# Splitting the first up-weight load over two queues in a state-space plus gated-MLP kernel

## The chip, the cores and the metric

The kernel runs on one core of a Trainium2 chip. The metric is device time in microseconds (us) of one execution; the figure for a kernel is the median of several runs. The core's engines are TensorE (PE in the profile, its weight loads PEld), VectorE (DVE), ScalarE (ACT), GpSimd (POOL) and SyncE (SP). DMA loads here are issued by SP and by ScalarE (SPq and ACTq in the profile).

## The reference

Everything is bfloat16 at the edges. For x of 2048 tokens by 512 channels:

```
xn = layernorm(x)                                   # per token, eps 1e-5
A  = S5(xn):  Bu = xn @ B_bar.T                     # complex, 512 states
              h[t] = Lam_bar * h[t-1] + Bu[t]       # a scan over 2048 tokens
              y = 2 * Re(h @ C.T) + xn * Dskip
B  = (gelu(xn @ w_gate) * (xn @ w_up)) @ w_down     # 512 -> 1376 -> 512
out = x + A + B
```

`Lam_bar` and `B_bar` are made from the small parameters `log_dt`, `Lambda_re` and `Lambda_im` (512 numbers each).

## The kernel before

Tokens are worked in four blocks of 512, a block in four tiles of 128. The program records every operation with the buffers that it reads and writes, and a planner (`Sched`) sets the order on VectorE, ScalarE and GpSimd from estimated durations. TensorE and SP keep the order in which the code records them. `emit` then writes out each engine's list with the semaphore waits. `order_behind(op, prev)` tells the planner to put `op` behind `prev`.

**The start.** Block 0 is treated specially, because weights and tokens arrive while it is worked. Its four x tiles are loaded one by one (`ld_x0`). The gate weights `WG` and up weights `WU` come in four chunks of columns (0 to 384, to 640, to 896, to 1376). The first gate chunk comes as two loads of 192 KB, for channels 0 to 255 and 256 to 511 (`ld_wg0`, line 490): the first on SP, the second on ScalarE's queue. The first up chunk is one load of 384 KB on SP. SP issues in this order: x of tile 0, gate half 0, x of tile 2, the up chunk, x of tile 3, then the other chunks, then the transpose of the parameters (`tr_par`, line 511), four transposes of block 0's normalised tiles (`TR(0)`, line 711), x of block 1, and the transposing loads of B. ScalarE's queue issues x of tile 1, gate half 1 and the three parameter loads (`load_par`, line 507), and then its first arithmetic: the mean of tile 1 (line 926).

**Work on block 0.** VectorE takes each tile's statistics and subtracts the mean (line 921, for tile 1 line 929 with ScalarE's mean). TensorE transposes the centred tile (`cent_T`, line 662), ScalarE (once VectorE too, if the letters say so) copies the transpose to memory (line 669). Then `GT_mm` (line 687) multiplies a tile by a part of the gate or up columns. Parts are 192, 192, 256 and 256 columns wide; part 0 and part 1 make up the first chunk. A product has four matmuls, one for each 128 channels (`ks`); `us` is [0] for gate, [1] for up. Gate and up of one part lie beside each other in one PSUM bank. `GT_evac` applies gelu with the tile's scale on ScalarE (line 696) and multiplies by the up half on VectorE (line 699).

For tiles 0 and 1 the order on TensorE is: gate of tile 0 for the first two channel blocks, both parts; the same for the last two; a few filler matmuls (line 909); gate of tile 1, both parts; up of tile 0 part 0; the transpose of tile 2; up of tile 0 part 1; up of tile 1, both parts. Tile 2 and the rest follow with gate and up together. ScalarE's list behind this has: gelu of tile 0 part 0, copy of tile 2's transpose, gelu of tile 0 part 1, and so on.

**The rest.** Blocks go through the gate and up products (`GU`, line 812), the input projection of the scan (`BU`, line 723), the scan and its rotations on VectorE (`CHAIN`), and the output products (`DN`, line 853). `BU(1)` follows `BU(0)` on TensorE and needs the four transposes of block 1.

Of the kernel before, what the change touches and what calls it, by code (L numbers as in the profile page):

```python
# [77 lines left out]
class Sched:  # L78
# [95 lines left out]
    def _backward(self, span):  # L174
        ops = self.ops
        left = {op.id: len(op.users) for op in ops}
        late = {op.id: span for op in ops}
        ready = {e: [] for e in ENGINES}
        last = {e: [op for op in ops if op.eng == e] for e in INORDER}
        for op in ops:  # L180
            if left[op.id] == 0 and op.eng not in INORDER:
                ready[op.eng].append(op)
        busy = {e: span for e in ENGINES}
        begin = {}
        n = len(ops)
        while n:
            best = None
            for e in ENGINES:
                if e in INORDER:
                    if not last[e] or left[last[e][-1].id]:  # L190
                        continue
                    op = last[e][-1]
                else:
                    if not ready[e]:
                        continue
                    op = max(ready[e], key=lambda o: (min(busy[e], late[o.id]), o.finish, o.id))
                end = late[op.id] if op.kind == "dma" else min(busy[e], late[op.id])
                if best is None or end > best[0]:
                    best = (end, op)
            end, op = best  # L200
            e = op.eng
            if e in INORDER:
                last[e].pop()
            else:
                ready[e].remove(op)
            begin[op.id] = end - op.dur
            if op.kind == "dma":
                begin[op.id] = min(begin[op.id], busy[e] - op.issue)
                busy[e] = begin[op.id]
            else:  # L210
                busy[e] = begin[op.id]
            n -= 1
            for d in op.deps:
                late[d.id] = min(late[d.id], begin[op.id] - LAT(d, op))
                left[d.id] -= 1
                if left[d.id] == 0 and d.eng not in INORDER:
                    ready[d.eng].append(d)
        return begin

    def _forward(self, prio):  # L220
        ops = self.ops
        free_at = {e: 0.0 for e in ENGINES}
        dma_pipe = 0.0
        ndeps = {op.id: len(op.deps) for op in ops}
        ready = {e: [] for e in ENGINES}
        queue = {e: [op for op in ops if op.eng == e] for e in INORDER}
        qpos = {e: 0 for e in INORDER}
        for op in ops:
            if ndeps[op.id] == 0 and op.eng not in INORDER:
                ready[op.eng].append(op)  # L230
        order = {e: [] for e in ENGINES}
        nleft = len(ops)

        def rdy_time(op):
            return max([d.finish + LAT(d, op) for d in op.deps] + [op.nb])

        while nleft:
            best = None
            for e in ENGINES:
                if e in INORDER:  # L240
                    if qpos[e] >= len(queue[e]):
                        continue
                    op = queue[e][qpos[e]]
                    if ndeps[op.id] != 0:
                        continue
                    st = max(free_at[e], rdy_time(op))
                else:
                    if not ready[e]:
                        continue
                    cands = [(max(free_at[e], rdy_time(op)), op) for op in ready[e]]  # L250
                    st0 = min(c[0] for c in cands)
                    stb, b = min(cands, key=lambda c: (prio[c[1].id], c[1].id))
                    if stb <= st0 + 150.0:
                        st, op = stb, b
                    else:
                        limit = max(stb, prio[b.id])
                        fill = [c for c in cands if c[1] is not b and
                                c[0] + (c[1].issue if c[1].kind == "dma" else c[1].dur) <= limit]
                        if fill:
                            f0 = min(c[0] for c in fill)  # L260
                            fill = [c for c in fill if c[0] <= f0 + 150.0]
                            st, op = min(fill, key=lambda c: (prio[c[1].id], c[1].id))
                        else:
                            st, op = stb, b
                if best is None or st < best[0]:
                    best = (st, op)
            st, op = best
            e = op.eng
            if e in INORDER:
                qpos[e] += 1  # L270
            else:
                ready[e].remove(op)
            op.start = st
            if op.kind == "dma":
                free_at[e] = st + op.issue
                xfer = op.dur - 2000.0
                t0 = max(st, dma_pipe) if xfer > 10.0 else st
                dma_pipe = max(dma_pipe, t0 + xfer)
                op.finish = t0 + xfer + 2000.0
            else:  # L280
                op.finish = st + op.dur
                free_at[e] = op.finish
            order[e].append(op)
            nleft -= 1
            for u in op.users:
                ndeps[u.id] -= 1
                if ndeps[u.id] == 0 and u.eng not in INORDER:
                    ready[u.eng].append(u)
        return order, max(op.finish for op in ops)

    def emit(self):
# [19 lines left out]
        for e in ENGINES:  # L311
            seen = {}
            prog = []
            for op in order[e]:
                need = {}
                for d in op.deps:
                    if d.kind == "eng" and d.eng == e and (e == "tensor" or d is op.behind):
                        continue
                    key = ("e", d.eng) if d.kind == "eng" else ("d", d.id)
                    if seen.get(key, 0) >= d.val:  # L320
# [35 lines left out]
def d_dve_ts4x(n): return 220.0 + 0.26 * n  # L356
D_TINY = 160.0
def d_act(n, ptr=0): return 190.0 + 0.833 * n + 90.0 * ptr
# [3 lines left out]
def build(nc, ins, out):  # L362
    with ExitStack() as es:
# [121 lines left out]

        def ld_x0(j, queue="sync", after=()):
            return S.dma(lambda e, j=j: e.dma_start(X[j].ap, x2[128 * j:128 * (j + 1), :]), 128 * 1024, writes=[X[j]], tag="ld_x0", queue=queue, after=after)
        WG0h = [Buf("WG0h%d" % n, "sbx", n / 2, (n + 1) / 2) for n in range(2)]

        def ld_wg0(n, queue, after=()):  # L490
            return S.dma(lambda e: e.dma_start(WG.ap[:, 2 * n:2 * n + 2, 0:384],
                                        ins["B_w_gate"][256 * n:256 * (n + 1), 0:384].rearrange("(k p) f -> p k f", p=128)),
                  192 * 1024, writes=[WG0h[n]], tag="ld_w", queue=queue, after=after)
        ld_x0(0)
        S.order_behind(ld_x0(1, "scalar", [wrm]), GATE["table"])
        ld_wg0(0, "sync")
        S.order_behind(ld_wg0(1, "scalar", [wrm]), GATE["table"])
        ld_x0(2)
        ld_w(WU, WUc, ins["B_w_up"], 0)
        ld_x0(3)  # L500
        for ci in (1, 2):
            ld_w(WG, WGc, ins["B_w_gate"], ci)
            ld_w(WU, WUc, ins["B_w_up"], ci)

        def load_par():
            for q, nm in enumerate(("A_log_dt", "A_Lambda_re", "A_Lambda_im")):
                S.dma(lambda e, q=q, nm=nm: e.dma_start(PROW.ap[4 * q:4 * q + 4, :], ins[nm].rearrange("(s p) -> s p", p=128)),
                      1024, writes=[PROWq[q]], tag="ld_" + nm, queue="scalar", after=[half])

        def tr_par():  # L510
            S.dma(lambda e: e.dma_start_transpose(PAR.ap.rearrange("p q t -> p (q t)").unsqueeze(1), PROW16.ap), 4096,
# [163 lines left out]
        def GT_mm(j, r, bank, us, ks=range(KD)):  # L675
# [1 line left out]
            w = f1 - f0  # L677
            ci = max(0, r - 1)
            Wc = [(WGc, WUc)[u][ci] for u in us]
            if ci == 0 and us == [0] and len(ks) == 2:  # L680
                Wc = [WG0h[ks[0] // 2]]
            dst = PS[bank][:, w * us[0]:w * (us[-1] + 1)].rearrange("p (w f) -> p w f", w=len(us))

            def f(e):
# [235 lines left out]
        def sub(j):  # L920
            return V(lambda e: e.tensor_scalar(XN[j].ap, X[j].ap, MVt[0][j].ap[:, 0:1], None, ALU.subtract),
                     d_dve_ts4x(512), [X[j], MVt[0][j]], [XN[j]], "sub")
        load_par()
        load_W()
        tr_par()
        ACT(lambda e: e.activation(H0[3].ap[:, 0:D], X[1].ap, ACTF.Copy, scale=-1.0 / D, accum_out=NM1.ap), d_act(512) + 90,
            [X[1]], [H0[3], NM1], "mean1")
        ch(*stats(0, 0)); ch(sub(0))
        ch(V(lambda e: e.tensor_scalar(XN[1].ap, X[1].ap, NM1.ap, None, ALU.add), d_dve_ts4x(512), [X[1], NM1], [XN[1]], "sub"))
        ch(*stats(0, 1))  # L930
# [24 lines left out]
            GT_evac(j, r, bank, rss[j])  # L955
        for r in range(2):
            GT_mm(1, r, ub[1, r], [0])
        for j in range(2):
            for r in range(2):
                GT_mm(j, r, ub[j, r], [1])  # L960
                GT_evac(j, r, ub[j, r], rss[j])
                if j == 0 and r == 0:
                    cent_T(2, tb)
# [100 lines left out]
```

## Time and profile before

| | us |
|---|---|
| median of 6 runs | 177.92 (177.64 to 178.01) |
| the profiled execution | 177.93 |
| its span, first to last instruction | 176.2 |
| TensorE busy | 172.8 (98%) |
| VectorE busy | 162.4 (92%) |
| ScalarE busy | 90.3 (51%) |
| GpSimd busy | 9.7 (6%) |

The profile lists instructions in time order (start and length in us, engine, source line, operation, tiles), with the idle time before one in brackets and what ended it. The chain is the sequence of work that ended last, followed back from the last instruction. A window row gives, for a stretch of time, its length, the busy time of PE, PEld, DVE, ACT and POOL (with instruction counts), the granted TensorE clock, the DMA share and GB/s. Matmuls overlap: one that is 0.25 us long can follow another after 0.08 us, so the distance of starts is what counts. Times below are from the start of the span.

### The profile page before, as it was taken

How to read it: one execution, taken by the hardware profiler on the slowest of the kernel's cores; microseconds unless marked ns; L12 is line 12 of the kernel's file. 1: busy time of each engine (PE TensorE's matmuls, PEld its weight loads, DVE VectorE, ACT ScalarE, POOL GpSimd, SP SyncE). 2: the span in 40 equal slices, each digit the busy share in tenths (PEclk: the TensorE clock that was granted, in tenths of full speed). 3: DMA queues.
4: the chain of work that ended last, by engine and by line, in shares of the span. 5: the costliest groups of instructions: out<-in, count | busy, mean ns of one | idle time of the engine just before them, and what ended most of it. 6: DMA issues, size and time to landing. Idle time of an engine off the chain costs nothing.

```text
span 176.2 us, 2489 instructions
## 1 busy us (share of the span) xinstructions
PE 172.8 (98%) x876; PEld 84.7 (48%) x891; DVE 162.4 (92%) x283; ACT 90.3 (51%) x169; POOL 9.7 (6%) x25
## 2 busy tenths in 40 slices
PE   8999999999999999999999999999999999999995
PEld 3854464444644444444644444444464444444454
DVE  6978999986999999979999999999999999999981
ACT  5476568899876899002676793000667790000000
POOL 3212030210000000011000000000000000000000
PEclk9999999999999999999999999999999999999999
DMA  5996996974997000012015000002101000000141
GB/s 162 316 311 152 207 234 130 133 139 102 240 290 165 4 0 0 2 41 78 4 34 113 4 0 0 4 0 77 42 0 30 4 0 0 0 0 0 33 149 61
DMA packets 33396, 14.36 MB, mean 81 GB/s; under 512 B 23688, under 2 KB 33384, under 8 KB 33384
## 3 DMA queue, kind: packets, MB, share of 16 engines
q1 hardware_dynamic: 32944, 13.87, 34.5%
q10 hardware_dynamic: 440, 0.33, 0.7%
q8 instruction: 7, 0.11, 0.3%
q14 instruction: 5, 0.04, 0.1%
HBM read 6.46 MB, written 2.10 MB: 49 GB/s over the span
## 4 chain that ended last, share of the span: by engine, by line
PE 98%; issue 0%; DVE 0%
PE PS L853 37%; PE PS L812 32%; PE PS L723 16%; PE PS L687 7%; PE PS L786 3%; PE PS L902 2%; PE PS L662 1%; PE PS L909 0%; DVE arena L871 0%
## 5 line engine op out<-in xcount | busy, mean ns | idle before, releaser
L853 PE MATMUL PS<-arena 128*128 128x512 bf16 (+3 forms) x317 | 65.9, 367 | 0.3
L812 PE MATMUL PS<-arena 128*128 128x512 bf16 x258 | 57.5, 380 | 0.3
L853 PEld LDWEIGHTS PS<-arena 128*128 128x128 bf16 (+1 forms) x323 | 30.8, 98 | 35.2
L812 PEld LDWEIGHTS PS<-arena 128*128 128x128 bf16 x264 | 25.8, 98 | 30.4
L756 DVE TENSOR_TENSOR_SCAN arena<-arena 128x512 bf16<-128x512 f32 x32 | 38.8, 1255 | 0.0
L827 ACT ACTIVATE arena<-PS 128x512 bf16<-128x512 f32 x33 | 19.8, 599 | 37.0 <-PE PS L812 33.4
L723 PE MATMUL PS<-arena 128*128 128x512 bf16 x125 | 27.8, 380 | 0.2
L831 ACT ACTIVATE arena<-PS 128x512 bf16<-128x512 f32 x33 | 19.7, 597 | 4.8 <-PE PS L812 4.6
L845 ACT ACTIVATE PS<-arena 128x512 f32<-128x512 bf16 (+2 forms) x17 | 9.6, 581 | 20.4 <-PE PS L853 19.7
L723 PEld LDWEIGHTS PS<-arena 128*128 128x128 bf16 x128 | 12.5, 98 | 14.9
L727 ACT ACTIVATE arena<-PS 128x512 bf16<-128x512 f32 x32 | 17.6, 594 | 2.3 <-PE PS L723 2.3
L871 DVE TENSOR_TENSOR arena<-PS,arena 128x512 bf16<-128x512 f32 (+2 forms) x17 | 10.8, 652 | 5.0 <-PE PS L853 4.5
L833 DVE TENSOR_TENSOR arena<-arena 128x512 bf16<-128x512 bf16 x33 | 13.0, 418 | 1.7 <-ACT arena L831 1.6
L687 PE MATMUL PS<-arena 128*128 128x192 bf16 (+2 forms) x80 | 13.2, 320 | 0.0
L613 DVE BATCH_NORM_STATS2 arena<-arena 128x6 f32<-128x512 bf16 x16 | 10.3, 684 | 0.8 <-DMA arena<-in_A_x_dram 0.8
L743 DVE TENSOR_TENSOR arena<-arena 128x4096 bf16<-128x4096 bf16 (+1 forms) x5 | 9.2, 1861 | 0.5 <-ACT arena L608 0.5
L687 PEld LDWEIGHTS PS<-arena 128*128 128x128 bf16 x80 | 7.3, 100 | 5.0 <-DMA arena<-in_B_w_up_dram 0.3
L745 DVE TENSOR_TENSOR arena<-arena 128x4096 bf16<-128x4096 bf16 (+1 forms) x5 | 9.2, 1859 | 0.4 <-ACT arena L609 0.4
L696 ACT ACTIVATE arena<-PS,arena 128x192 bf16<-128x192 f32 (+1 forms) x16 | 6.7, 447 | 5.0 <-PE PS L687 4.2
L768 DVE TENSOR_TENSOR arena<-arena 128x4096 bf16<-128x4096 bf16 x4 | 9.2, 2289 | 0.1
L769 DVE TENSOR_TENSOR arena<-arena 128x4096 bf16<-128x4096 bf16 x4 | 9.1, 2285 | 0.0
L699 DVE SCALAR_TENSOR_TENSOR arena<-PS,arena 128x192 bf16<-128x192 f32 (+1 forms) x16 | 6.6, 444 | 0.9 <-ACT arena L696 0.7
(84 smaller groups left out, 110.4 us busy)
## 6 DMA issues: line engine op xcount, KB each, us to landing
out_dram<-arena SPq DMA_DIRECT2D x15, 128.0 KB, 1.7
arena<-in_A_x_dram SPq DMA_DIRECT2D x3, 512.0 KB, 4.9
arena<-in_B_w_down_dram SPq DMA_DIRECT2D x1, 1280.0 KB, 8.1
arena<-in_B_w_gate_dram SPq DMA_DIRECT2D x2, 256.0 KB, 5.6
arena<-in_B_w_up_dram SPq DMA_DIRECT2D x2, 256.0 KB, 5.8
arena<-in_B_w_gate_dram SPq DMA_DIRECT2D x1, 480.0 KB, 5.8
arena<-in_B_w_up_dram SPq DMA_DIRECT2D x1, 480.0 KB, 5.9
arena<-arena SPq DMA_TRANSPOSE x25, 2.5
```

The costliest lines, as they stand in the source:

```text
L613: return (V(lambda e: e.bn_stats(ST[tt].ap, X[tt].ap), d_dve_1x(512), [X[tt]], [ST[tt]], "bnst"), V(lambda e: e.bn_aggr(MVt[b][j].ap, ST[t ...
L687: ins_ = e.matmul(dst, XCd(j, k), WGU[:, us[0]:us[-1] + 1, k, f0:f1], start=(k == 0), stop=(k == KD - 1))
L723: ins_ = e.matmul(PS[bank][:, :], BBT[c][dk].ap[:, 128 * s:128 * (s + 1)], XNT[b].ap[:, dk, :], start=(dk == 0), stop=(dk == KD - 1))
L727: GATE["evBu"] = ACT(lambda e, bank=bank, k3=k3, s=s, c=c: e.activation(SSc[k3][s][c].ap, PS[bank][:, :], ACTF.Copy), d_act(512), [BANK[ba ...
L756: V(lambda e, g=g, rb=rb, init=init: e.tensor_tensor_scan(g.ap, rb, g.ap, init, ALU.mult, ALU.add), d_dve_scan(512), [g, PA[RRr]] + ([CARc ...
L812: ins_ = e.matmul(PS[bank][0:m, c0:c1], W.ap[:, dk, 128 * ft:128 * ft + m], XNT[b].ap[:, dk, c0:c1], start=(dk == 0), stop=(dk == KD - 1))
L827: GATE["last_gelu"] = ACT(lambda e, bg=bg, kk=kk, m=m: e.activation(GG[kk].ap[0:m, :], PS[bg][0:m, :], ACTF.Gelu_apprx_tanh), d_act(512), ...
L831: ACT(lambda e, bu=bu, kk=kk, m=m: e.activation(UPB[kk].ap[0:m, :], PS[bu][0:m, :], ACTF.Copy), d_act(512), [BANK[bu]], [UPB[kk]], "evU")
L833: V(lambda e, kk=kk, m=m, ft=ft, k2=k2: e.tensor_tensor(HTt[k2][ft].ap[0:m, :], GG[kk].ap[0:m, :], UPB[kk].ap[0:m, :], ALU.mult), d_dve_tt ...
L845: ACT(lambda e: e.activation(PS[bank][:, c0:c1], X[tt].ap[:, c0:c1], ACTF.Copy), d_act(c1 - c0), [X[tt]], [BANK[bank]], "seed")
L853: ins_ = e.matmul(PS[bank][:, c0:c1], l_[:, 128 * j:128 * (j + 1)], r_[:, c0:c1], start=False, stop=last and n == len(ops) - 1, skip_group ...
L871: V(lambda e: e.tensor_tensor(OUTB[ko].ap[:, c0:c1], PS[bank][:, c0:c1], XD[tt].ap[:, c0:c1], ALU.add), d_dve_1x(c1 - c0), [BANK[bank], XD ...
```

## The change

The first up chunk is loaded in two halves like the gate chunk: channels 256 to 511 on ScalarE's queue behind the gate half, channels 0 to 255 on SP where the whole chunk was. The three parameter loads are ordered one behind the other and behind the mean of tile 1, which is therefore recorded first. Up products of tile 0 are recorded in halves that each wait for their own load: the first two channel blocks for both parts, then the last two of part 0, the transpose of tile 2, and the last two of part 1. The planner and `emit` learn that an operation behind a DMA of its own queue follows its issue, not its landing, and needs no wait.

As built, ScalarE's list is: x of tile 1, gate half 1, up half 1, mean of tile 1, `log_dt`, three copies of transposes, `Lambda_re`, `Lambda_im`, gelu of tile 0 part 0. SP's list differs only in the size of the up load. On VectorE one small parameter operation (line 559) and one product (line 699) change places. TensorE's list differs only in the up products of tile 0.

```diff
 # in _backward, _forward and emit of Sched
-                late[d.id] = min(late[d.id], begin[op.id] - LAT(d, op))
+                late[d.id] = min(late[d.id], begin[op.id] + d.dur - d.issue if d is op.behind and d.kind == "dma" else begin[op.id] - LAT(d, op))
...
-            return max([d.finish + LAT(d, op) for d in op.deps] + [op.nb])
+            return max([d.start + d.issue if d is op.behind and d.kind == "dma" else d.finish + LAT(d, op) for d in op.deps] + [op.nb])
...
-                    if d.kind == "eng" and d.eng == e and (e == "tensor" or d is op.behind):
+                    if d.eng == e and (d is op.behind or d.kind == "eng" and e == "tensor"):
...
 # loads
-        WG0h = [Buf("WG0h%d" % n, "sbx", n / 2, (n + 1) / 2) for n in range(2)]
-
-        def ld_wg0(n, queue, after=()):
-            return S.dma(lambda e: e.dma_start(WG.ap[:, 2 * n:2 * n + 2, 0:384],
-                                        ins["B_w_gate"][256 * n:256 * (n + 1), 0:384].rearrange("(k p) f -> p k f", p=128)),
-                  192 * 1024, writes=[WG0h[n]], tag="ld_w", queue=queue, after=after)
+        WG0h, WU0h = ([Buf("W%s0h%d" % (nm, n), "sbx", o + n / 2, o + (n + 1) / 2) for n in range(2)] for nm, o in (("G", 0), ("U", 100)))
+
+        def ld_w0(W, Wh, src, n, queue, after=()):
+            return S.dma(lambda e: e.dma_start(W.ap[:, 2 * n:2 * n + 2, 0:384],
+                                        src[256 * n:256 * (n + 1), 0:384].rearrange("(k p) f -> p k f", p=128)),
+                  192 * 1024, writes=[Wh[n]], tag="ld_w", queue=queue, after=after)
+        ld_wg0 = lambda *a: ld_w0(WG, WG0h, ins["B_w_gate"], *a)
+        ld_wu0 = lambda *a: ld_w0(WU, WU0h, ins["B_w_up"], *a)
         ld_x0(0)
         S.order_behind(ld_x0(1, "scalar", [wrm]), GATE["table"])
         ld_wg0(0, "sync")
         S.order_behind(ld_wg0(1, "scalar", [wrm]), GATE["table"])
+        S.order_behind(ld_wu0(1, "scalar", [wrm]), GATE["table"])
         ld_x0(2)
-        ld_w(WU, WUc, ins["B_w_up"], 0)
+        ld_wu0(0, "sync")
         ld_x0(3)
...
         def load_par():
+            last = GATE["mean1"]
             for q, nm in enumerate(("A_log_dt", "A_Lambda_re", "A_Lambda_im")):
-                S.dma(lambda e, q=q, nm=nm: e.dma_start(PROW.ap[4 * q:4 * q + 4, :], ins[nm].rearrange("(s p) -> s p", p=128)),
-                      1024, writes=[PROWq[q]], tag="ld_" + nm, queue="scalar", after=[half])
+                last = S.order_behind(S.dma(lambda e, q=q, nm=nm: e.dma_start(PROW.ap[4 * q:4 * q + 4, :], ins[nm].rearrange("(s p) -> s p", p=128)),
+                      1024, writes=[PROWq[q]], tag="ld_" + nm, queue="scalar", after=[half]), last)
...
 # in GT_mm
-            if ci == 0 and us == [0] and len(ks) == 2:
-                Wc = [WG0h[ks[0] // 2]]
+            if ci == 0 and len(us) == 1 and len(ks) == 2:
+                Wc = [(WG0h, WU0h)[us[0]][ks[0] // 2]]
...
 # the order in which block 0 is recorded
-        load_par()
         load_W()
+        GATE["mean1"] = ACT(lambda e: e.activation(H0[3].ap[:, 0:D], X[1].ap, ACTF.Copy, scale=-1.0 / D, accum_out=NM1.ap), d_act(512) + 90,
+            [X[1]], [H0[3], NM1], "mean1")
+        load_par()
         tr_par()
-        ACT(lambda e: e.activation(H0[3].ap[:, 0:D], X[1].ap, ACTF.Copy, scale=-1.0 / D, accum_out=NM1.ap), d_act(512) + 90,
-            [X[1]], [H0[3], NM1], "mean1")
...
         for r in range(2):
             GT_mm(1, r, ub[1, r], [0])
+        for r in range(2):
+            GT_mm(0, r, ub[0, r], [1], (0, 1))
         for j in range(2):
             for r in range(2):
-                GT_mm(j, r, ub[j, r], [1])
+                GT_mm(j, r, ub[j, r], [1], range(KD) if j else (2, 3))
                 GT_evac(j, r, ub[j, r], rss[j])
                 if j == 0 and r == 0:
                     cent_T(2, tb)
```

More of the change, by code (lines that the diff above doesn't have):

```diff
@@ L922, in sub @@
                      d_dve_ts4x(512), [X[j], MVt[0][j]], [XN[j]], "sub")
+        load_W()
+        GATE["mean1"] = ACT(lambda e: e.activation(H0[3].ap[:, 0:D], X[1].ap, ACTF.Copy, scale=-1.0 / D, accum_out=NM1.ap), d_act(512) + 90,
+            [X[1]], [H0[3], NM1], "mean1")
         load_par()
-        load_W()
         tr_par()
-        ACT(lambda e: e.activation(H0[3].ap[:, 0:D], X[1].ap, ACTF.Copy, scale=-1.0 / D, accum_out=NM1.ap), d_act(512) + 90,
-            [X[1]], [H0[3], NM1], "mean1")
         ch(*stats(0, 0)); ch(sub(0))
```

## The prediction

> **What bounds the kernel now.** I read the page first, then the chain that ended last in order of time, then the timelines of the first 10 us, where all of the change lies.
>
> ```profile
> span 176.2 us, 2489 instructions
> ...
> PE 172.8 (98%) x876; PEld 84.7 (48%) x891; DVE 162.4 (92%) x283; ACT 90.3 (51%) x169; POOL 9.7 (6%) x25
> ...
> PE 98%; issue 0%; DVE 0%
> ```
>
> The chain is TensorE alone. Between 7.25 us and its last matmul at 174.1 us the matmuls follow each other without a gap (the repeated gap of 0.05 us in the chain, every 10.8 us, is one matmul missing from the record: there the distance between two starts is two regular ones). So time can be won only where TensorE idles before 7.25 us, and any later work that comes late to it costs its lateness.
>
> ```profile
> 6.33 0.23 PE PS L909 x4
> 6.56 0.66 PE PS L687 x8
> 7.22 0.03 issue
> 7.25 0.50 PE PS L687 x4
> 7.76 0.22 PE PS L662 x4
> ```
>
> The eight gate matmuls of tile 1 have a pitch of 0.66/8 = 0.082 us. Then the first up matmul stands at 7.25. How long TensorE waited is seen better in the two timelines (start, length, engine):
>
> ```profile
> 6.40 1.36 PE L687 MATMUL PS<-arena 128*128 128x192 bf16 x12
> ```
>
> ```profile
> 7.25 0.28 PEld L687 LDWEIGHTS PS<-arena 128*128 128x128 bf16 x4 [0.26 <-DMA arena<-in_B_w_up_dram]
> ```
>
> Twelve matmuls from 6.40 to 7.76: the last is 0.247 long, so eleven steps take 1.11 us, and at 0.082 they would take 0.90. About 0.20 us is idle before 7.25, and the weight load names the first up chunk. That is all that the change can win on TensorE. The load was issued on SP at 2.16 and takes 5.0 us to land, so 7.2.
>
> ScalarE's first work on tiles 0 to 2 is the second thing to look at:
>
> ```profile
> 1.43 0.45 ACTq L491 DMA_DIRECT2D arena<-in_B_w_gate_dram  x1
> 1.92 0.61 ACTq L507 DMA_DIRECT2D arena<-in_A_log_dt_dram  x1
> ...
> 2.87 0.31 ACTq L507 DMA_DIRECT2D arena<-in_A_Lambda_im_dram  x1
> 3.28 0.63 ACT L926 ACTIVATE arena<-arena 128x512 bf16<-128x512 bf16 x1 [1.06 <-DMA arena<-in_A_x_dram]
> ...
> 7.86 0.42 ACT L696 ACTIVATE arena<-PS,arena 128x192 bf16<-128x192 f32 x1 [1.87 <-PE PS L687]
> 8.18 0.59 ACT L669 ACTIVATE arena<-PS 128x512 bf16<-128x512 bf16 x1
> ```
>
> The gelu of tile 0, part 0 (7.86) waits for the up matmuls of that part; behind it in order comes the eviction of tile 2's transpose (8.18 to 8.77), and TensorE's next matmuls, those of tile 2, start at 8.82. This place has no slack: TensorE's own pitch would have brought it there at 8.81.
>
> SP's queue is the third:
>
> ```profile
> 4.84 1.53 SPq L483 DMA_DIRECT2D arena<-in_B_w_up_dram  x1
> 6.41 1.23 SPq L483 DMA_DIRECT2D arena<-in_B_w_gate_dram  x1
> 7.68 0.69 SPq L483 DMA_DIRECT2D arena<-in_B_w_up_dram  x1
> 8.50 1.33 SPq L511 DMA_TRANSPOSE arena<-arena  x1
> 9.88 5.18 SPq L711 DMA_TRANSPOSE arena<-arena  x4
> 15.11 0.58 SPq L477 DMA_DIRECT2D arena<-in_A_x_dram  x1
> ```
>
> From 4.84 to 22.4 it issues back to back. The transpose of the parameters (8.50) waits for all three parameter loads, and everything behind it moves with it.
>
> **The change part by part.** Durations are those of the profiled execution: 177.93 us, a span of 176.2 and 1.73 around it; the median of the runs is 177.92, so one stands for the other.
>
> *Up chunk in two loads.* The same bytes in two loads. ScalarE issues one more load (0.45 us, like the gate half's) at 1.92 in place of the parameters; SP's issue of 0.43 becomes about 0.41, and that is lost in the later issues of 1.53 and 1.23, which against 0.43 to 0.58 for the same kind before them contain waits of their own. What counts is when both halves are there. At 4.25 us the packet records have some 56 KB of tile 2's x on SP's ring and 69 KB of the gate half on ScalarE's still to move; each ring then has a 197 KB half behind it: 252 against 265 KB. With both rings busy the engines carried no more than with one:
>
> ```profile
> 4.50:5.00 0.50, 0.50 (x7) 0.50 (x6) 0.50 (x2) 0.25 (x1) 0.00 (x0) 1.00 0.99 288
> ...
> 6.50:7.00 0.50, 0.50 (x10) 0.49 (x6) 0.47 (x3) 0.00 (x0) 0.00 (x0) 1.00 1.10 310
> ```
>
> (last column GB/s; 4.5 to 5.0 has both queues, 6.5 to 7.0 SP's alone.) So the two halves share what one load had, and the later of the two lands about when the whole one did. Bounds: 6.7, where 15 of the 16 engines had finished the whole load by the trace's semaphore events, and 7.2, where the last had. I take 7.15, near the upper end, because the total of bytes ahead of the second half is the same.
>
> The Trainium skill, "DMA: Bandwidth & Descriptors", section "Issuing engines are not separate DMA queues", speaks against this edit: loads from two issuing engines run on the same 16 DMA engines, and only issue time is saved. By that rule alone both halves would be there at 7.2 and the sum below would end at +0.16; by the rows' lower bound of 6.7 it would end at -0.04.
>
> *Order of the up matmuls.* Tile 0 now runs: first halves of part 0 and part 1 (2+2 matmuls), second half of part 0 (2), transpose of tile 2 (4), second half of part 1 (2). TensorE's count is unchanged and so is its pitch. But the gelu of part 0 now stands behind six up matmuls, not four: 2 x 0.082 = 0.16 us later after the first. With T the start of the first up matmul: before, T = 7.25 and the gelu at T + 0.61; after, T + 0.77 (0.01 less if nothing stalls it). The eviction of tile 2 follows 0.32 later, and TensorE's tile 2 matmuls 0.64 after that. If both halves are there by 7.0, T = 7.06 and the tile 2 matmuls start at 8.78 against 8.82: a gain of 0.04, not 0.20; the rest is a new idle of 0.17 us at 8.6, behind ScalarE. If T stays 7.25 they start at 8.98: a loss of 0.16. With the first half at 7.15, T = 7.2 and the loss is 0.1.
>
> *Tile 2's x.* It shares the engines longer, since ScalarE's ring no longer empties at 5.3. It landed at 5.71 (VectorE's statistics start at 5.73); the 0.37 us that it had alone after the gate half doubles, so it comes up to 0.37 later; at the other end 0. VectorE then delivers tile 2 at 7.03 to 7.4. The transpose of tile 2 is due on TensorE at 7.55 to 7.7, the reciprocal (7.11, then 7.48) is due at the gelu, 7.8 or later. Covered; cost 0, and if the delay were 0.8 us it would be about 0.1.
>
> *Parameters behind tile 1's mean.* The mean starts at 3.28 because x of tile 1 lands at 3.26, not because of the issues before it (they end at 3.18): gain 0, and VectorE is busy until 4.18 anyway. The issues now cost ScalarE 0.61 after 3.3, covered until its eviction at 4.75, and 0.28 + 0.31 after 5.4, covered until 7.8. The landing is what matters. The last parameter was issued at 2.87 and landed at 6.76 by the semaphore events; SP asked for it at 8.43: 1.7 us of cover. Now it is issued at about 5.75, behind the up half. From the issue-to-landing rows on this queue, 2.3 us (x of tile 1) to 3.9 us (gate half), it lands between 8.05 and 9.65. I take 8.2: in the profile the three small loads took 1.7 to 2.1 us from the first one's first packet to the last landing, and the up half should be through at 6.0 to 6.4 on the quicker engines (an estimate: the whole load landed there between 5.8 and 6.4). Cost 0.
>
> *The rest.* One small VectorE operation (0.16 us, parameters) changes place with a hidden product at 15.1 to 15.5; the bank it frees is wanted some 2 us later: 0. ScalarE and SP otherwise keep their order.
>
> Sum: +0.1 for the up halves, 0 elsewhere: 177.93 + 0.1 = 178.0.
>
> **The rivals.** *The parameters come late (slower).* SP's transpose of them slips, and with it x of block 1 (issued 15.11, landed 19.01; VectorE's statistics start at 19.03, without slack), its normalisation and the four transposes of it from 24.56:
>
> ```profile
> 24.56 5.14 SPq L711 DMA_TRANSPOSE arena<-arena  x4
> ```
>
> The last lands at 31.66 by the semaphore events, and TensorE loads the weights of block 1's input projection at 31.77, on time for its matmul at 31.97: slack 0.1 us. A parameter landing at 8.43 + s costs s - 0.1. It decides the verdict from a landing of about 8.9 on, where s - 0.1 passes 0.36. At 9.65 s is 1.2 and the time 179.0; in the middle, 9.2, it is 178.6. For it: three serial loads behind a half that has 16 packets per engine; against it: 8.2 above.
>
> *The stall simply goes.* Both halves by 7.0, the gelu no obstacle: 177.93 - 0.20 = 177.73; with the gelu, 177.89. Both are within what can be told. Against it: the same bytes on the same engines. Faster by more needs idle time that this trace does not show.
>
> *Tile 2's x is over 1 us late*, because ScalarE's ring gets the larger share: the transpose of tile 2 and its eviction slip, some 0.3 to 0.5: 178.2 to 178.4.
>
> **How the numbers follow.** About 0.2% (0.36 us) is what a measurement of this kernel can tell from no change; the runs before span 0.37 us. Forecast case (177.9 to 178.1) 0.44, all within. Late parameters 0.31, of which 0.26 are slower by more than 0.36. The stall goes 0.18, of which 0.07 for a gain beyond the visible idle. Late x of tile 2 0.07, 0.03 of it beyond. So faster 0.07, same 0.64, slower 0.29. The likeliest case's own range is 177.85 to 178.15. The range for 8 in 10 takes in the gain of the stall and the late parameters up to their upper middle: 177.7 to 178.8.
>
> **What would show it.** Right: in the new profile the weight load of the first up matmul still waits for an up half, until 7.1 to 7.25; the gelu of tile 0 starts 0.77 us after it; a weight load ahead of tile 2's matmuls waits about 0.17 us for ScalarE near 8.7; from there TensorE has no gap. Wrong: the first up matmul at 7.06 and no wait at 8.7; or SP's parameter transpose later than 8.6 and a weight load near 32 us that waits for a DMA; or statistics of tile 2 after 6.3.

## The result and the profile after

The changed kernel takes 178.9 us (median of 20 runs, 177.93 to 179.44) against 177.91 for the kernel before on the same chip (43 runs, 177.43 to 178.48). The ratio is 1.0056, with a 95% interval of 1.0046 to 1.0065: 0.56% slower, some 1.0 us. The profiled execution took 178.79 us.

The page of the changed kernel, with the row of its chain, answers to the first lines shown of before:

```profile
span 177.0 us, 2490 instructions
...
PE 172.7 (98%) x876; PEld 84.4 (48%) x891; DVE 162.0 (92%) x283; ACT 89.7 (51%) x169; POOL 10.1 (6%) x25
...
PE 82%; DMA 8%; DVE 6%; issue 1%; POOL 1%; ACT 1%; SPq 0%; DVEq 0%; POOLq 0%
```

TensorE is busy as long as before; it now idles in places, so the chain no longer runs through it alone. The chain in order of time names what it waits for (start, length, what):

```profile
4.78 0.91 ACT arena L673 x3
5.72 4.39 DMA arena<-in_A_Lambda_im_dram
10.21 3.31 DMA arena<-arena
...
17.48 3.80 DMA arena<-in_A_x_dram
...
30.20 2.47 DMA arena<-arena
32.81 6.21 PE PS L727 x28
```

It goes from ScalarE's copies to the issue of the last parameter, `Lambda_im`, at 5.72; that takes 4.39 us to land. Then come the transpose of the parameters, x of block 1 and the transposes of block 1, and TensorE takes over at 32.81. The rows left out are mostly VectorE's, from 13.66 to 17.13 behind the parameters; SP's own issues stand back to back there too (below), and E11 shows that SP's order is what held x of block 1. (Of the lines named here, those above 500 are the old ones plus 4.) The two queues show the issues:

```profile
3.30 0.52 ACTq L511 DMA_DIRECT2D arena<-in_A_log_dt_dram  x1
...
5.37 0.32 ACTq L511 DMA_DIRECT2D arena<-in_A_Lambda_re_dram  x1
5.72 0.35 ACTq L511 DMA_DIRECT2D arena<-in_A_Lambda_im_dram  x1
```

```profile
10.21 1.17 SPq L515 DMA_TRANSPOSE arena<-arena  x1
11.44 6.00 SPq L715 DMA_TRANSPOSE arena<-arena  x4
17.48 0.58 SPq L477 DMA_DIRECT2D arena<-in_A_x_dram  x1
...
26.34 5.13 SPq L715 DMA_TRANSPOSE arena<-arena  x4
```

The parameters' transpose went out at 8.50 before and at 10.21 now, x of block 1 at 15.11 and 17.48, the first transpose of block 1 at 24.56 and 26.34. TensorE, in its matmuls of the two stretches concerned:

```profile
19.02 5.13 PE L816 MATMUL PS<-arena 128*128 128x512 bf16 x23 [0.49 <-DVE arena L703]
...
32.81 2.54 PE L727 MATMUL PS<-arena 128*128 128x512 bf16 x11 [0.44 <-DMA arena<-arena]
```

The first is `GU(0)`, which reads all of block 0's transposed tiles; the row names VectorE, which freed a bank, but by the semaphore events the last of those tiles landed at 18.67 (16.28 before) and the weight load follows at 18.77. The second is `BU(1)`, for which the last transpose of block 1 landed at 32.68 (31.66 before). And at the start, in the weight loads:

```profile
7.57 0.81 PEld L691 LDWEIGHTS PS<-arena 128*128 128x128 bf16 x10
8.62 0.60 PEld L691 LDWEIGHTS PS<-arena 128*128 128x128 bf16 x5 [0.24 <-ACT arena L673]
```

The wait for the up chunk at 7.25 is gone (the halves landed at 6.39 and 6.71 by the semaphore events), and a wait for ScalarE's copy has come at 8.6.

An account of TensorE's lost time makes this one sum. For each pair of matmuls I took the distance of their starts less the regular pitch, left out the places where a record is missing, and added them up by stretch (us, one profiled execution each; E1, E2, E7 and E11 are experiments below):

| | 4.1 to 6.95 | up wait, near 7.2 | near 8.6 | near 18 | near 32 | last matmul starts |
|---|---|---|---|---|---|---|
| before | 0.87 | 0.20 | 0 | 0 | 0 | 174.13 |
| after | 0.71 | 0 | 0.18 | 0.43 | 0.61 | 174.96 |
| E2: parameters late, nothing else | 0.51 | 0 | 0 | 0 | 0.75 | 174.32 |
| E1: after, parameters early | 1.01 | 0 | 0.18 | 0 | 0 | 174.25 |
| E7: after, parameters behind the mean | 1.02 | 0.09 | 0.18 | 0 | 0 | 174.34 |
| E11: after, x of block 1 first | 1.23 | 0.12 | 0.18 | 0 | 0 | 174.56 |

Between before and after the columns differ by 1.93 - 1.07 = 0.86, and the last matmul by 0.83. The first column is the stretch in which matmuls go over from half to full rate, with the waits for the gate halves in it; it differs between executions whatever the kernel (more below), and the medians are the better guide to sizes.

### The profile page after: what moved, and what is told of

It is laid out like the page before. It is cut to its first block, busy times and chain, and to the rows that moved or that the text cites. A ratio compares the mean times of both kernels' runs of the same rounds, so it can differ in the third digit from the quotient of the medians.

```text
span 177.0 us, 2490 instructions
## 1 busy us (share of the span) xinstructions
PE 172.7 (98%) x876; PEld 84.4 (48%) x891; DVE 162.0 (92%) x283; ACT 89.7 (51%) x169; POOL 10.1 (6%) x25
## 4 chain that ended last, share of the span: by engine, by line
PE 82%; DMA 8%; DVE 6%; issue 1%; POOL 1%; ACT 1%; SPq 0%; DVEq 0%; POOLq 0%
PE PS L857 37%; PE PS L816 29%; PE PS L727 12%; DMA arena<-arena 3%; DMA arena<-in_A_Lambda_im_dram 2%; PE PS L790 2%; DMA arena<-in_A_x_dram 2%; PE PS L906 2%; DVE arena L606 1%; DVE arena L703 1%; DVE arena L617 1%; DVE arena L636 1%; POOL arena L559 1%; ACT arena L673 1%; DVE arena L837 0%
```

## The experiments

All of them move operations in the lists that the planner has left, and touch nothing else, so that no other order changes. `move(engine, ops, place)` takes operations out of one engine's list and puts them back at `place`; the waits are written out after it. `par` is the list of the three parameter loads, `mean1` tile 1's mean, `evT` the copies of the transposes on ScalarE, `tr_par` the transpose of the parameters on SP. In the texts written beforehand, theory A says that the loss runs from the late parameters through SP to block 1; A1, A2 and C are causes for the late landing: A1 that SP's own long issues hold it up, A2 that the small loads wait for their turn on busy DMA engines, C that a load lands only after what the other queue was given before it. Other letters name rivals that the texts themselves describe.

**E2, the kernel before with its parameter loads where the changed kernel has them.**

```diff
         S.schedule()
+        move("scalar", par[:1], behind(mean1))
+        move("scalar", par[1:], behind(evT[2]))
```

> The kernel before with one part of the change alone: the three parameter loads stand on ScalarE's queue where the changed kernel has them (log_dt behind tile 1's mean, Lambda_re and Lambda_im behind the third copy). The up chunk stays one load and TensorE's order stays. Theory A (the late parameter loads hold SP's queue; block 1's transposes, and perhaps block 0's, then come late to TensorE): SP issues the parameters' transpose at 9.5 to 10.5 us, not 8.5; TensorE waits 0.4 to 0.6 us near 32 us for a DMA; the time is 178.6 to 179.1. Theory B (the split load and TensorE's new order cost the time): the transpose stays near 8.5 and the time at 177.9.

178.54 us against 177.83, ratio 1.0041 (1.0028 to 1.0054). The up chunk is one load here and TensorE's order is that of before. SP's queue, and TensorE where it waits:

```profile
9.30 1.18 SPq L511 DMA_TRANSPOSE arena<-arena  x1
10.53 5.99 SPq L711 DMA_TRANSPOSE arena<-arena  x4
16.56 0.58 SPq L477 DMA_DIRECT2D arena<-in_A_x_dram  x1
...
25.66 5.15 SPq L711 DMA_TRANSPOSE arena<-arena  x4
```

```profile
32.17 3.18 PE L723 MATMUL PS<-arena 128*128 128x512 bf16 x14 [0.58 <-DMA arena<-arena]
```

The parameters alone bring 0.7 of the 1.0 us (the two intervals overlap), with the same wait at block 1's transposes. SP's issue, the wait of 0.75 near 32 and the time stand just outside the ranges expected. `Lambda_im` is issued at 5.24 here and lands at 9.21, 0.91 earlier than in the changed kernel, and block 0's last transpose lands at 17.78: there is no wait near 18.

**E1, the changed kernel with its parameter loads ahead of the mean again.**

```diff
         S.schedule()
+        move("scalar", par, ahead(mean1))
```

> The changed kernel with the parameter loads put back ahead of tile 1's mean; the split up chunk and TensorE's new order stay. Theory A: SP issues the parameters' transpose by 8.5 us, no wait at 18 or 32 us; the mean starts 0.3 us later (3.6), tile 1 is up to 0.2 later, the new wait of 0.18 near 8.6 stays: 177.8 to 178.1. Theory B: 178.7 to 179.0 as in the changed kernel.

177.97 against 177.83, ratio 1.0007 (0.999 to 1.0025). SP's transpose of the parameters goes out at 8.21, and no wait is left near 18 or 32:

```profile
8.21 1.26 SPq L515 DMA_TRANSPOSE arena<-arena  x1
```

So the loss comes with the parameters and goes with them. What is left of the change, the two loads and the order on TensorE, can't be told from no change.

**E7, all three directly behind the mean; E9, one alone late.** These ask how late is too late. E7 keeps the order that the change gives (behind the mean), but without the three copies in between; E9 moves only `Lambda_im` in the kernel before.

```diff
 # E7, on the changed kernel
         S.schedule()
+        move("scalar", par, behind(mean1))
 # E9, on the kernel before
         S.schedule()
+        move("scalar", par[2:], behind(evT[2]))
```

> The changed kernel, with all three parameter loads directly behind tile 1's mean (issued 3.3 to 4.3 us), none behind the copies. The earlier runs make theory C the first: a load issued on ScalarE's queue, however small, lands only when what SP issued before it has moved (Lambda_im issued at 5.66 landed at 9.54, with the last weight chunk issued before it at 9.32, although SP was not held). By C the last parameter lands between 7.9 and 8.7, SP issues the parameters' transpose at 8.0 to 8.8, no wait at 18 us, at most 0.2 at 32 us: 177.7 to 178.1. If three small loads in a row behind the up half were slow by themselves (theory D), the last lands at 9.5 or later and the time stays near 178.8.

> The kernel before, with Lambda_im alone moved behind the third copy (issued at about 5.4). Theory C: it waits for what SP issued before 5.4 and lands at 8.9 to 9.8; the parameters' transpose is issued at 9.0 to 9.9; TensorE waits 0.3 to 0.7 near 32 us; 178.3 to 178.8. Theory D (three loads in a row are slow): one alone on an empty queue lands by 7.9, the transpose stays at 8.5, and the time at 177.9.

E7: 177.95 against 177.96, ratio 1.0001 (0.9989 to 1.0014). Its last parameter was issued at 4.17 and landed at 8.47, in time for SP:

```profile
4.17 0.42 ACTq L511 DMA_DIRECT2D arena<-in_A_Lambda_im_dram  x1
```

```profile
8.56 1.19 SPq L515 DMA_TRANSPOSE arena<-arena  x1
```

E9: 178.27 against 177.96, ratio 1.0023 (1.0009 to 1.0038). One load of 1 KB, issued at 5.36 and landed at 9.76:

```profile
5.36 0.26 ACTq L507 DMA_DIRECT2D arena<-in_A_Lambda_im_dram  x1
```

```profile
9.85 1.18 SPq L511 DMA_TRANSPOSE arena<-arena  x1
```

It is not the number of small loads in a row: one alone, with the other two issued 2.8 us before it, takes 4.4 us. Nor is it the place behind the mean: E7 has that and loses nothing. It is the issue behind the three copies, 1.5 us later, that costs. In E9's profiled execution TensorE itself was late at the start (1.31 us lost between 4.1 and 6.95) and had no wait at 32, so the 0.3 us stand on the median and not on a row.

**E8, fewer loads on SP between the issue and the landing.** In the changed kernel SP's issues of 1.78 and 0.77 us stand around the parameters. E8 puts SP's last three weight chunks behind the transpose of the parameters.

```diff
         S.schedule()
+        move("sync", tagged("sync", "ld_w")[5:], behind(tr_par))
```

> Why the late loads take 4.4 us to land. The changed kernel, with SP's last three weight chunks issued behind the parameters' transpose, so that SP has no issue of over 0.6 us before it; the DMA engines still have the earlier chunks to move until about 9.5. Theory A1 (descriptors of ScalarE's small loads queue behind SP's weight loads while those wait for room): the small loads issued at 5.4 and 5.7 land by 8.0, and the parameters' transpose is issued at 7.7 to 8.2. Theory A2 (they wait for their turn on busy engines): they land at 9.3 or later, and the transpose is issued at 9.4 or later. The time itself tells little, since later weights delay block 0's transposes by about 1 us: 177.9 to 179.

180.15, ratio 1.0147 (1.0096 to 1.0197), above the 177.9 to 179 expected: the weights that were moved come late. SP's queue and ScalarE's:

```profile
4.17 0.51 SPq L483 DMA_DIRECT2D arena<-in_B_w_gate_dram  x1
9.64 1.18 SPq L515 DMA_TRANSPOSE arena<-arena  x1
```

```profile
5.66 0.30 ACTq L511 DMA_DIRECT2D arena<-in_A_Lambda_im_dram  x1
```

SP issues nothing from 4.68 until the parameters are there, and `Lambda_im` still lands only at 9.54, with the weight chunk issued at 4.17, which lands at 9.32. A1 falls: no long issue of SP is needed. A2 and C are left.

**E12, less ahead of the parameters.** The direct turn of E8: five weight chunks are taken away instead of three, so that at 5.7 SP has been given 512 KB less than in E8.

```diff
         S.schedule()
+        move("sync", tagged("sync", "ld_w")[3:], behind(tr_par))
```

> The changed kernel with less on SP's queue ahead of the parameters: its last five weight chunks are issued behind the transpose of the parameters. Lambda_im is still issued at about 5.7 on ScalarE's queue, with one 256 KB weight chunk of SP's (issued 3.15) and x of tile 3 ahead of it. Theory C (a load lands only after what the other queue was given before it): the three parameters land within 0.5 us of that chunk, Lambda_im at 7.6-8.4 in place of 10.12, and SP's transpose of them is issued at 7.7-8.5. Theory that the delay belongs to these small loads or to ScalarE's queue, whatever SP has ahead (about 3.9-4.4 us from issue to landing): 9.6-10.1 as in the changed kernel. The time says nothing: the weights come too late for TensorE, and 181-185 is expected.

```profile
3.15 0.43 SPq L483 DMA_DIRECT2D arena<-in_B_w_gate_dram  x1
7.96 1.18 SPq L515 DMA_TRANSPOSE arena<-arena  x1
```

```profile
5.73 0.30 ACTq L511 DMA_DIRECT2D arena<-in_A_Lambda_im_dram  x1
```

The same issue time, and the landing at 7.86 in place of 10.12; SP's transpose 2.25 us earlier. Taking bytes from SP's queue makes a 1 KB load on ScalarE's land earlier. This does not tell C from A2; the packet records below speak for C. (181.80 in one run: the weights are late here.) In eight kernels, all by the semaphore events, the load lands with the chunks that SP was given 0.5 to 2.6 us before it:

| | `Lambda_im` issued | landed | weight chunks of SP landing around it (issued, landed) |
|---|---|---|---|
| E12 | 5.73 | 7.86 | 3.15, 8.13 (its last) |
| E7 | 4.17 | 8.47 | 3.15, 8.58; 3.62, 9.18 |
| E8 | 5.66 | 9.54 | 4.17, 9.32 (its last) |
| E2 | 5.24 | 9.21 | 3.66, 8.66; 4.21, 9.50 |
| E9 | 5.36 | 9.76 | 3.67, 9.26; 4.22, 10.09 |
| E4 | 5.67 | 9.81 | 4.18, 9.52; 4.79, 10.32 |
| E11 | 5.75 | 10.09 | 3.63, 9.50; 4.19, 10.32 |
| after | 5.72 | 10.12 | 4.18, 9.58; 4.73, 10.39 |

C holds in this looser form only: in seven of the eight (all but E8) a chunk that SP was given before the load lands after it.

**E4, the parameters' transpose put behind block 0's on SP.** If only SP's order carries the delay, taking the waiting instruction out of the way should cure it.

```diff
         S.schedule()
+        move("sync", [tr_par], behind(tagged("sync", "tr_x0")[3]))
```

> The changed kernel, with the parameters' transpose issued on SP behind block 0's four transposes, not ahead of them. The parameter loads are as late as in the changed kernel, but less stands behind them. Theory A: block 0's transposes start near 8.1 and wait for nothing but VectorE's norms (11.2 to 11.6), x of block 1 is issued at 15 or before, TensorE waits neither at 18 nor at 32 us: 177.8 to 178.1. Theory B: 178.7 to 179.0.

179.67, ratio 1.0095 (1.0072 to 1.0117): worse than the change, and the expectation was wrong. SP did what was asked, and VectorE shows why it did not help:

```profile
7.92 5.64 SPq L715 DMA_TRANSPOSE arena<-arena  x4
13.68 1.73 SPq L515 DMA_TRANSPOSE arena<-arena  x1
15.46 0.58 SPq L477 DMA_DIRECT2D arena<-in_A_x_dram  x1
```

```profile
17.83 0.16 DVE L560 TENSOR_TENSOR arena<-arena 128x4 f32<-128x4 bf16 x1 [3.32 <-POOL arena L559]
...
21.66 0.69 DVE L617 BATCH_NORM_STATS2 arena<-arena 128x6 f32<-128x512 bf16 x1
```

Block 0's transposes and x of block 1 (landed 19.31) are early now, but VectorE keeps its own order: its first work on the parameters waits until 17.83, and block 1's statistics stand behind it at 21.66, later than the 21.31 of the changed kernel. TensorE waits 1.28 us near 32. The parameters are a dependency of two queues, SP's and VectorE's, and I had followed one.

**E11, x of block 1 ahead of the parameters' transpose.** This moves one thing out of the way instead: the parameters stay late, and VectorE's wait for them stays.

```diff
         S.schedule()
+        move("sync", [x for x in S.order["sync"] if x.tag == "ld_x1"], ahead(tr_par))
```

> The changed kernel with one issue moved: SP issues the load of x of block 1 ahead of the transpose of the parameters, so that it no longer stands behind the wait for them; the parameters themselves stay late. Theory C with the path as read (late parameters, then SP in order, then x of block 1, its statistics, the four transposes of block 1, TensorE at 32): x of block 1 lands before 14 in place of 21.29, the last transpose of block 1 lands by 31.9, TensorE's wait near 32 (0.61 us in the changed kernel) is under 0.15, and the time falls by about that, from 178.9 to 178.2-178.5; what stays is the wait near 18 (0.43) behind the transposes of block 0, which move with the parameters still. If the 0.61 near 32 hangs on something else than x of block 1 (SP's own issues, or the transposes of block 0), the wait stays at 0.4 or more and the time at 178.7-179.0.

178.28 against 177.92, ratio 1.0034 (1.0012 to 1.0056).

```profile
8.65 0.75 SPq L477 DMA_DIRECT2D arena<-in_A_x_dram  x1
10.18 1.18 SPq L515 DMA_TRANSPOSE arena<-arena  x1
11.41 5.18 SPq L715 DMA_TRANSPOSE arena<-arena  x4
...
25.78 5.13 SPq L715 DMA_TRANSPOSE arena<-arena  x4
```

```profile
18.79 5.06 PEld L816 LDWEIGHTS PS<-arena 128*128 128x128 bf16 x24
...
32.23 2.87 PEld L727 LDWEIGHTS PS<-arena 128*128 128x128 bf16 x14 [0.15 <-issue]
```

The time fell as expected and the wait near 32 is gone (0.15 us at the weight load, none in the matmuls). Three details were wrong: x landed at 15.33, not before 14, the last transpose of block 1 at 32.12, not by 31.9, and the wait near 18, which I had thought would stay, went too. There the four transposes of block 0 were issued without the issue of 2.09 us that the changed kernel has at 14.04, and the last landed at 17.79 in place of 18.67. By the table's first columns TensorE also came there 0.64 later than in the changed kernel, and either was enough to end a wait of 0.43. Why that issue is long in one kernel and not in the other isn't settled (E2 has one of 2.07 us at 14.44). What remains of E11's loss has an interval from 0.2 to 1.0 us, and no row in its profile beyond the 0.18 near 8.6 and the start, so its cause stays open.

**E3 and E10, the new wait near 8.6.** E3 is E7 with TensorE's old order (the up matmuls of part 1's first half back behind tile 2's transpose); E10 is E7 with ScalarE's copy of tile 2 ahead of the first gelu.

```diff
 # E3, E7's move and
+        up = tagged("tensor", "GT")[6:10]
+        move("tensor", up[1:2], ahead(up[3]))
 # E10, E7's move and
+        move("scalar", evT[3:4], ahead(gelu[0]))
```

> Parameters directly behind the mean, the up chunk in two loads, but TensorE's order of before (all four up matmuls of part 0, the transpose of tile 2, then part 1). If the new wait comes from the two matmuls of part 1 that now stand ahead of part 0's last two, it is gone (at most 0.02), the first gelu is 0.16 earlier against the first up matmul, and with both halves landed by 7.0 the time is 177.6 to 177.9. If the second half lands after 7.1, TensorE waits for it at 7.2 instead and the time is 177.8 to 178.1.

> Parameters directly behind the mean as in the run before it, and ScalarE copies tile 2's transpose ahead of the first gelu, not behind it. If the wait of 0.18 us near 8.6 is the copy standing behind that gelu, it goes, and the first gelu is later by 0.3 with nobody waiting: 0.1 to 0.2 less than with the parameters moved alone, 177.6 to 177.9. If TensorE waits there for the transpose itself, nothing changes.

E3: 177.82 against 177.96, ratio 1.0004 (0.9988 to 1.002). E10: 178.13, ratio 1.0006 (0.9989 to 1.0023), where 177.6 to 177.9 was expected. In both the wait is gone. In E10, weight loads and ScalarE:

```profile
7.38 1.83 PEld L691 LDWEIGHTS PS<-arena 128*128 128x128 bf16 x17
```

```profile
7.64 0.60 ACT L673 ACTIVATE arena<-PS 128x512 bf16<-128x512 bf16 x1 [2.00 <-PE PS L666]
8.13 1.45 ACT L700 ACTIVATE arena<-PS,arena 128x192 bf16<-128x192 f32 x4
```

The weight loads run through, where E7 and the changed kernel have 0.24 us of idle weight loading ahead of tile 2. So the wait is the copy behind the gelu, as the prediction had it. But no gain over E7 can be told: 0.18 us is a tenth of a per cent, about the half-width of these intervals. No version that was tried is faster than the kernel before.

## Why the prediction was wrong

It said 178.0 with no measurable change; the time is 178.9, slower, and just above the end of its range (178.8). Its own steps, one by one:

- *Parameters behind tile 1's mean: the step that failed.* "I take 8.2 ... Cost 0." The last parameter landed at 10.12, beyond even the upper bound of 9.65, and SP, which had asked for it at 8.43 before, was held until 10.21. The bounds were rows of issue-to-landing times on the same queue (2.3 and 3.9 us), as though the queue set them, and 8.2 was near the lower one. The nearest rows were the parameter loads themselves: before the change they took 3.3 to 3.9 us (issued at 1.92, 2.56 and 2.87, landed at 5.53, 5.88 and 6.76), which puts the landing at 9.1 to 9.6. Measured, `Lambda_im` took 4.40. E8 and E9 ruled out SP's long issues and the number of loads, and E12 showed what sets the landing: the bytes that SP's queue was given before. The prediction had the figure for that in hand: SP's weight chunks issued up to 4.84 landed up to 10.9 in the trace of before, so that a load issued among them could be expected to land among them.
- *The rival "parameters come late" was the case.* Its path (SP, x of block 1, its statistics, the four transposes, TensorE at 32) is the chain after, and E1, E2 and E11 show it by undoing, doing and cutting it. Its price was too high: s = 10.12 - 8.43 = 1.69 gives 1.59 by its rule of s - 0.1, and TensorE started the matmul that needs block 1's transposes 0.84 late (32.81 against 31.97). The delay shrinks on its way. x of block 1 landed 2.28 late, the transposes of it went out 1.78 late, and their last landed 1.02 late: VectorE needed 5.0 us in place of 5.5 between the statistics and the first transpose, and the transposes 6.34 in place of 7.10 from issue to landing. TensorE was itself 0.25 late by then (by the table's columns up to 18), and 1.02 less this and the 0.1 of slack leaves 0.67, where 0.61 was measured. The prediction had also missed that block 0's transposes, behind the same wait, could make TensorE wait: 0.43 near 18. By the chain, which does not run through that wait, it is not lost on top: without it TensorE would have waited longer near 32, as in E2 (0 and 0.75). It took the issue of 2.09 us as well: that is 0.83 longer than the 1.26 of the issue behind it, more than the whole wait.
- *Up chunk in two loads.* "I take 7.15"; the later half landed at 6.71, by its lower bound, and TensorE did not wait. But neither did it in E2's and E9's profiles, where the chunk is one load (landed 6.66 and 7.24), while in E7 and E11 with the halves (7.25 and 7.48) it waited 0.09 and 0.12. The 0.20 us that seemed to be there to win belonged to that one execution as much as to the kernel. That the split itself brings nothing measurable was right (E1, E7).
- *Order of the up matmuls.* For halves there by 7.0 it had the stall gone and a new idle of 0.17 behind ScalarE at 8.6. Measured: 0.18 near 8.6, and E10 and E3 confirm the cause.
- *Tile 2's x.* Up to 0.37 later was allowed for; it landed at 5.43, not later than before (5.71). Cost 0 was right.
- *The sum.* It had +0.1 for the up halves and 0 elsewhere. In the two profiled executions the up halves come to -0.20 + 0.18 = -0.02, and the late parameters to 0.43 + 0.61 = 1.04. With -0.16 in the first stretch that makes 0.86, the difference between these two executions (178.79 and 177.93); the medians differ by 0.99.

## What to carry to other kernels

When a small load is moved later on a quiet queue, price its landing by what the other queues have been given shortly before it, and read that off the landings of the big loads issued around the same time, not off earlier loads of the same queue. Then list every in-order queue that waits for it (here SP and VectorE both), and everything behind it there: a 1 KB load moved by 3 us behind the weights cost more than the stall that the change set out to remove. And before a stall of 0.2 us is taken as time to win, see it in a second execution.

## What the runs showed of the hardware that was not expected

*Two queues served about in order of issue.* The packet records of the changed kernel show that the late landing is a late start. The parameters are 12 packets of 256 bytes on ScalarE's queue. Four start between 5.67 and 6.28 (`log_dt`), and eight between 8.89 and 9.52. From 6.3 to 8.8 ScalarE's queue starts no packet at all, while from 6.5 on SP's starts 240 to 340 weight packets in each half microsecond. In E12 the same eight start between 6.58 and 7.10. The Trainium skill, "DMA: Bandwidth & Descriptors", section "Queues, rings and completion order", has each DMA engine take turns between the queues that have work, packet by packet; by that rule alone, with their descriptors at the DMA engines, the eight would have started soon after their issue at 5.4 and 5.7. The packets show another order, and the measurement decides: here a load of 1 KB waited for three of the four 256 KB chunks that the other queue had been given before it (the fourth, issued at 4.73, landed after it). Where the order is made, ahead of the DMA engines or in them, isn't settled by these runs.

*TensorE's start.* Matmuls run at half rate at first (0.107 us from start to start for 128 columns, then 0.056), and the change to full rate came between about 3.5 us (E10) and 6.7 us (E9), at 4.3 in E2, at 5.75 in the profile of before and by 5.3 in that of after, in executions whose instructions on TensorE up to there are alike. The filler matmuls ahead of tile 1's last gate products show it, in E10 and then in E11:

```profile
5.83 0.39 PE L913 MATMUL PS<-const-bfloat16-1.0 128*128 128x128 bf16 x4
```

```profile
6.52 0.39 PE L913 MATMUL PS<-const-bfloat16-1.0 128*128 128x128 bf16 x4
```

0.69 us apart, and the loss between 4.1 and 6.95 was 0.52 and 1.23. The granted clock in the window rows reads 1.00 all the same (as in the row 4.50:5.00 that the prediction shows). The Trainium skill, "TensorE: Matmul & The Clock Gate", section on the clock gate (Part 1), says that the window which opens the clock runs free of the kernel, so that the number of slow matmuls differs from run to run. The rows agree that it differs; that the window is the reason, no run here shows. The difference is why single executions vary by several tenths of a microsecond, and an early full rate only makes TensorE wait at 32 (E2: 0.51 lost at the start, 0.75 there) when a transfer sets the pace.
